# Loading q one head at a time: four transfers of 32 partitions instead of two of 64

## The chip, the cores and the metric

One core of one Trainium2 chip runs the kernel. The metric is the device time of one launch in microseconds (us), the median over several runs. All inputs and the output are float32 in the chip's HBM.

## The reference

With q, k, v of shape 8 x 8 x 576 x 64 (batch, head, position, head dimension):

```
kv  = einsum('bhsd,bhse->bhde', k, v)
out = einsum('bhsd,bhde->bhse', q, kv)
out = out / sqrt(mean(out * out, axis=-1) + 1e-6) * g_norm
x   = out with the heads side by side: 4608 x 512
h   = x @ w_in                       # 512 x 2048
g   = h * tanh(softplus(h))          # "mish"
result = g @ w_out                   # 2048 x 512
```

So there is a linear attention without a softmax, a norm over each head's 64 numbers, and a feed-forward part of two large products.

## The kernel before

The 4608 tokens are cut into nine tiles of 512 (`BLOCKS`, tile j). As a batch entry has 576 positions, a tile does not line up with the batches: `segments(j)` gives one segment (batch, first position, columns of the tile) for the tiles 0 and 8, and two for the tiles 1 to 7.

The work has two parts. In the first, tile after tile, TensorE multiplies x with w_in (L734 in tile 0, L780 later, products in a Strassen-like scheme of seven products a group; `gf` holds the x forms that are split into a high and a low part, `wfa` and `wfb` the same of w_in). ScalarE applies mish, and the results go by GpSimd's DMA queue to a buffer in HBM (`gd`, L818). In the second part, from about 531 us, they are read back and multiplied with w_out (L1148), and the result is stored.

While the products of tile j run, the attention of tile j + 1 is made in between. Its steps for each of two units u (four heads each):

- load (L452): q of the unit's four heads goes into `qs`, 128 partitions x 1024 numbers: a head takes 32 partitions, and a partition holds, for each segment, a run of consecutive numbers of its head. Unit 0 and unit 1 have a buffer each, which is free again when it has been transposed.
- transpose (L470): VectorE turns blocks of 32 x 32, `qs` into `fl` (unit 0) and `fm` (unit 1).
- project (L862): TensorE multiplies with the kv matrices of the batches (`kv`), made from k and v (loads `km`, `vm`, L344; products L371).
- square, sums, ln, exp: the norm, per token and head, into `fl`; keep (L567) and spread (L574) send it through HBM (`rd`) and back to all partitions of a head (`fh`, `fa`); normalize (L584) multiplies.
- the x forms (L200, L201) are made from that, and the next tile's products read them.

Between these steps the first tiles hold the conversion of w_in (load L242, scale L215, join L210 to L212, blocks and forms L200, L201) and the later ones that of w_out (load L224, stored again by GpSimd's queue, `wod`). Tile 0's q is loaded in another way (L432) and is not touched.

The order is written by hand: `WHEN`, `LATER`, `LATER0` and `LAST` give each step a slot among TensorE's products, and within each engine and each queue the instructions are issued in that order. All loads shown here, of q, k, v, the weights and the spread, are issued by SyncE (SP), one after the other; GpSimd's queue has the stores to `gd` and `wod`. An engine that waits for one instruction's input holds back all that stands behind it.

Of the kernel before, what the change touches and what calls it, by code (L numbers as in the profile page):

```python
# [36 lines left out]
def linear_attention_rms_mish_ffn(  # L37
# [34 lines left out]
    nc = tc.nc  # L72
    B, H, S, D = q.shape
# [4 lines left out]
    R = 32  # L78
# [20 lines left out]
    def start(j):  # L99
        return FIRST + NS * (j - 1) if j else 0  # L100
# [247 lines left out]
    def half(o, turned=False):  # L348

        o = 1 - o if turned else o  # L350
        return slice(o * D, (o + 1) * D)
# [33 lines left out]
    def quarter(p, m):  # L385
        return slice((2 * p + m) * R, (2 * p + m + 1) * R)
# [23 lines left out]
    def segments(j):  # L410

        segs, at_ = [], OFF[j]
        while at_ < OFF[j] + TS[j]:
            b, s0 = divmod(at_, S)
            n = min(S - s0, OFF[j] + TS[j] - at_)
            segs.append((b, s0, slice(at_ - OFF[j], at_ - OFF[j] + n)))
            at_ += n
        return segs
# [18 lines left out]
    def unit_steps(j, u):  # L437
# [4 lines left out]
        def load():  # L442


            t = qs[u] = att.tile([P, TM // R * D], F32, name=f"qs{u}")
            for b, s0, cols in segments(j):
                run = (cols.stop - cols.start) // R * D
                c0 = cols.start // R * D
                for o in range(2):
                    src = q[b, 4 * u + o, s0:s0 + 1, :]  # L450
                    src = bass.AP(src.tensor, src.offset, [[2 * S * D, 2], [run, R], [1, run]])
                    nc.sync.dma_start(t[half(o, u == 1), c0:c0 + run], src)  # L452

        def transpose(a=None):
            if j < T32:
# [130 lines left out]
        def projected():  # L586
            st["x2"] = x2_new()
            return st["x2"], st["q"]

        return {f.__name__: f for f in (projected, load, transpose, turned, project, square, scaled, sums, table, ln, exp, rstd, keep, spread, normalize)}  # L590


# [390 lines left out]
    for b in range(4, B):  # L983
        t = start(b - 2)
# [165 lines left out]
    def o_dst(st, block):  # L1150
        if "o" not in st:
            st["o"] = u_room("r", False, 2 * T).rearrange("p (r n) -> p r n", r=2)
        r, c = int(block[0]) - 1, int(block[1]) - 1
        return st["o"][:, r, c * G:(c + 1) * G]
# [77 lines left out]
    for i in range(NT):  # L1232
        for n in range(NQ):
            st = {"i": i, "n": n, "chunks": (2 * n, 2 * n + 1), "bank": bank_new, "take": nc.vector.tensor_copy if T32 <= i < NT - 1 and n in BY_DVE else nc.scalar.copy}
            t = start(i) + (7 if i else 8) * n
# [3 lines left out]
    t = start(NT)  # L1239
# [89 lines left out]
    o = o_dst(prev, "21")  # L1329
# [39 lines left out]
```

## Time and profile before

| | |
|---|---|
| median of 3 runs | 885.72 us (885.11 to 886.43) |
| the profiled execution | 887.06 us, its span 885.2 us |
| mean granted clock of TensorE | 0.958 |
| TensorE busy | 809.8 us, 91% of the span |
| VectorE busy | 595.6 us, 67% |
| ScalarE busy | 444.9 us, 50% |
| GpSimd busy | 109.1 us, 12% |
| DMA | 157.99 MB, mean 178 GB/s |

The profile is of one execution. Engines are named PE (TensorE's matmuls), PEld (its weight loads), DVE (VectorE), ACT (ScalarE), POOL (GpSimd) and SP (SyncE); a q behind the name means the engine's queue or sequencer. L452 is line 452 of the kernel, `qs<-in_q_dram` an instruction that writes qs and reads the input q, x60 the count. Times in rows of the timeline count from the start of the span. In a table of stretches, a row has the stretch, its length, the busy time of each engine with the number of instructions, the clock that TensorE was granted (1.00 is full speed), the mean busy share of the core's 16 DMA engines, and what these moved in GB/s.

### The profile page before, as it was taken

How to read it: one execution, taken by the hardware profiler on the slowest of the kernel's cores; microseconds unless marked ns; L12 is line 12 of the kernel's file. 1: busy time of each engine (PE TensorE's matmuls, PEld its weight loads, DVE VectorE, ACT ScalarE, POOL GpSimd, SP SyncE). 2: the span in 40 equal slices, each digit the busy share in tenths (PEclk: the TensorE clock that was granted, in tenths of full speed). 3: DMA queues.
4: the chain of work that ended last, by engine and by line, in shares of the span. 5: the costliest groups of instructions: out<-in, count | busy, mean ns of one | idle time of the engine just before them, and what ended most of it. 6: DMA issues, size and time to landing. Idle time of an engine off the chain costs nothing.

```text
span 885.2 us, 16602 instructions
## 1 busy us (share of the span) xinstructions
PE 809.8 (91%) x6764; PEld 730.4 (83%) x6764; DVE 595.6 (67%) x795; ACT 444.9 (50%) x688; POOL 109.1 (12%) x195
## 2 busy tenths in 40 slices
PE   7847879499897998889799999999999999999997
PEld 5635769489797997889689999888888888888887
DVE  3827754457554666474555489888888888788875
ACT  5626646164454655465364485454444544444452
POOL 2200101013131132233121110000000000000000
PEclk9977989799998999999899999999999999999999
DMA  9845815548476485656534996333334443343331
GB/s 305 284 140 187 249 62 162 180 147 296 171 272 216 157 271 176 199 179 240 179 108 157 360 315 265 117 121 127 133 121 138 169 145 119 120 143 120 126 113 49
DMA packets 63653, 157.99 MB, mean 178 GB/s; under 512 B 7384, under 2 KB 28120, under 8 KB 61272
## 3 DMA queue, kind: packets, MB, share of 16 engines
q1 hardware_dynamic: 49336, 109.92, 37.9%
q0 software_dynamic: 14144, 46.93, 14.2%
q8 instruction: 53, 0.87, 0.4%
q14 instruction: 24, 0.20, 0.1%
q10 hardware_dynamic: 96, 0.07, 0.0%
HBM read 100.40 MB, written 56.49 MB: 177 GB/s over the span
## 4 chain that ended last, share of the span: by engine, by line
PE 67%; DMA 24%; DVE 3%; SPq 3%; issue 1%; ACT 1%; DVEq 0%; POOL 0%; ACTq 0%
PE a L1148 21%; PE bc L1148 16%; PE a L780 14%; DMA qs<-in_q_dram 12%; PE bc L780 9%; DMA wfb<-in_moe_w_in_dram 7%; PE x L862 2%; PE q L1267 2%; DMA fh<-rd 2%; SPq L452 2%; DMA fa<-rd 1%; PE x L371 1%; DMA w<-in_moe_w_in_dram 1%; DMA gd<-u 1%; PE x L532 1%
## 5 line engine op out<-in xcount | busy, mean ns | idle before, releaser
L780 PE MATMUL a<-gf,wfb 128*128 128x256 f32 x1152 | 153.7, 288 | 2.3 <-DVE u L836 2.2
L200 ACT CAST gf<-g 128x1024 fp32r<-128x1024 f32 (+1 forms) x103 | 105.9, 1044 | 96.1 <-PE a L1148 50.5
L201 DVE TENSOR_TENSOR gf<-g,gf 128x1024 fp32r<-128x1024 f32 (+1 forms) x103 | 123.6, 1213 | 43.9 <-ACT gf L200 43.9
L780 PEld LDWEIGHTS a<-gf,wfb 128*128 128x128 f32 x1152 | 147.1, 197 | 5.6 <-DVE u L836 3.0
L1148 PE MATMUL a<-wfb,gf 128*128 128x512 f32 (+1 forms) x800 | 144.9, 337 | 0.0
L1148 PEld LDWEIGHTS a<-wfb,gf 128*128 128x128 f32 x800 | 125.4, 190 | 16.4
L1148 PE MATMUL bc<-wfb,gf 128*128 128x512 f32 (+1 forms) x544 | 98.0, 337 | 0.0
L1148 PEld LDWEIGHTS bc<-wfb,gf 128*128 128x128 f32 x544 | 82.6, 190 | 10.1
L818 POOL DMA_DIRECT2D gd<-u x96 | 57.0, 596 | 273.0 <-ACT u L197 228.5
L197 ACT ACTIVATE u<-u 128x1024 f32<-128x1024 f32 (+1 forms) x65 | 54.8, 843 | 69.9 <-DVE u L836 69.4
L836 DVE TENSOR_TENSOR u<-bc,u 128x512 f32<-128x512 f32 x64 | 43.1, 685 | 34.7 <-PE bc L780 30.2
L780 PE MATMUL a<-gf,wfa 128*128 128x256 f32 x384 | 54.7, 294 | 11.7 <-ACT u L694 11.7
L780 PEld LDWEIGHTS a<-gf,wfa 128*128 128x128 f32 x384 | 50.4, 200 | 17.4 <-ACT u L694 12.3
L780 PE MATMUL bc<-gf,wfa 128*128 128x256 f32 x384 | 53.9, 291 | 6.5 <-DVE u L836 4.2
L780 PEld LDWEIGHTS bc<-gf,wfa 128*128 128x128 f32 x384 | 50.2, 198 | 8.4 <-DVE u L836 4.7
L780 PE MATMUL bc<-a,wfb 128*128 128x256 f32 x384 | 52.5, 287 | 0.9 <-ACT u L686 0.9
L780 PE MATMUL bc<-gf,wfb 128*128 128x256 f32 x384 | 51.4, 283 | 0.0
L780 PEld LDWEIGHTS bc<-a,wfb 128*128 128x128 f32 x384 | 49.4, 196 | 2.3 <-issue 1.2
L1148 PE MATMUL bc<-wfa,gf 128*128 128x256 f32 (+1 forms) x272 | 50.3, 337 | 0.0
L1148 PE MATMUL a<-wfa,gf 128*128 128x256 f32 (+1 forms) x272 | 49.8, 336 | 0.0
L1148 PEld LDWEIGHTS a<-wfa,gf 128*128 128x128 f32 x272 | 44.1, 189 | 6.6
L780 PEld LDWEIGHTS bc<-gf,wfb 128*128 128x128 f32 x384 | 48.4, 192 | 0.1
(203 smaller groups left out, 1182.9 us busy)
## 6 DMA issues: line engine op xcount, KB each, us to landing
g<-gd SPq DMA_DIRECT2D x18, 2048.0 KB
gd<-u POOLq DMA_DIRECT2D x72, 256.0 KB, 5.6
gd<-u POOLq DMA_DIRECT2D x36, 512.0 KB, 6.7
w<-in_moe_w_out_dram SPq DMA_DIRECT2D x32, 256.0 KB
km<-in_k_dram SPq DMA_DIRECT2D x28, 288.0 KB
vm<-in_v_dram SPq DMA_DIRECT2D x28, 288.0 KB
wfb<-in_moe_w_in_dram SPq DMA_DIRECT2D x28, 256.0 KB
out_dram<-u SPq DMA_DIRECT2D x44, 128.0 KB
```

Source lines behind the costliest of these rows:

```text
L197: nc.scalar.activation(o, i, AF.Mish)
L200: nc.scalar.copy(hi, src)
L201: nc.vector.tensor_sub(lo, src, hi.bitcast(F32))
L371: nc.tensor.matmul(outs[a][half(o, a == 1)], kt[half(o), d], vt[half(o), d], start=(c == 0), stop=(c == 8))
L452: nc.sync.dma_start(t[half(o, u == 1), c0:c0 + run], src)
L532: nc.tensor.matmul(ss[j][hp * R:(hp + 1) * R, c], sel, sq[j, n][:, a, c], start=True, stop=True)
L780: nc.tensor.matmul(bank[:, jj], w[:, a, kc, :], xf[:, b, kc, :], start=first and jj == kc == s == 0, stop=(kc == 1 and s == 2), skip_group ...
L818: eng.dma_start(to, o)
L836: nc.vector.tensor_add(o, bank, o)
L862: nc.tensor.matmul(x2[half(o), a, cols], kvt[b % 2][r, m, u], of[r, c, m], start=m == 0, stop=m == 1)
L1148: nc.tensor.matmul(to, of, by, start=first and n == 0, stop=n == len(todo) - 1, skip_group_check=True)
L1267: nc.tensor.matmul(banks[b][:, h], gf[:, a, c, :], wo_form(2 * n + c, right)[:, :, d, :], start=n == c == s == h == 0, stop=last_one, skip ...
```

## The change

From the second tile on (tiles 1 to 8; tile 0 keeps its own load), a unit's four heads were loaded by two transfers for each segment, each of two heads into 64 partitions. Its source pattern has the two heads outermost, then 32 runs, then the numbers of a run. Now there are four transfers for each segment, one for each head, into 32 partitions each; the source pattern has the 32 runs outermost, which lie one behind the other in memory. The places in `qs` are the same: `half` gives 64 partitions, `quarter(p, m)` the m-th 32 of half p. The bytes are the same, too; the number of transfers of this line goes from 60 to 120, each of half the bytes.

```diff
             for b, s0, cols in segments(j):
                 run = (cols.stop - cols.start) // R * D
                 c0 = cols.start // R * D
-                for o in range(2):
-                    src = q[b, 4 * u + o, s0:s0 + 1, :]
-                    src = bass.AP(src.tensor, src.offset, [[2 * S * D, 2], [run, R], [1, run]])
-                    nc.sync.dma_start(t[half(o, u == 1), c0:c0 + run], src)
+                for h in range(4):
+                    src = q[b, 4 * u + h, s0:s0 + 1, :]
+                    src = bass.AP(src.tensor, src.offset, [[run, R], [1, run]])
+                    nc.sync.dma_start(t[quarter(h % 2 ^ u, h // 2), c0:c0 + run], src)
```

## The prediction

> **What bounds the kernel now.** I read the page first. Of its strips (40 slices of 22.1 us), the one of the granted clock and the one of DMA show that the second half is quiet: there TensorE runs at full clock, one matmul after the other. What can be won lies in the first 450 us, and there the chain of waits names one load again and again.
>
> ```profile
> span 885.2 us, 16602 instructions
> ...
> PE a L1148 21%; PE bc L1148 16%; PE a L780 14%; DMA qs<-in_q_dram 12%; PE bc L780 9%; DMA wfb<-in_moe_w_in_dram 7%; PE x L862 2%; PE q L1267 2%; DMA fh<-rd 2%; SPq L452 2%; DMA fa<-rd 1%; PE x L371 1%; DMA w<-in_moe_w_in_dram 1%; DMA gd<-u 1%; PE x L532 1%
> ```
>
> 12% of the chain is the load of q into qs, the very line of the change, and 2% its issue (SPq L452). The chain says what ended last, not what is lost; so next the waits (engine and line, what it waited for, us in all, times, longest):
>
> ```profile
> PE x L862 <- DVE fm L470: 21.9, 5, 5.4
> ...
> DVE fm L470 <- DMA qs<-in_q_dram: 12.5, 3, 6.4
> ...
> DVE fm L470 <- DMA w<-in_moe_w_out_dram: 11.2, 2, 6.2
> ```
>
> Five times TensorE stands still before the projection (L862), 21.9 us in all, because VectorE has not transposed the second q tile (fm). L470 reads nothing but qs, so whatever name stands behind it (a wait is put down to the last event), the load of q is what is late; VectorE takes its work in order and everything behind L470 waits too. The timeline shows three more stalls of that root (start, duration, engine, line, and in brackets the idle time before):
>
> ```profile
> 49.97 1.12 ACT L215 ACTIVATE wfa<-wfb 128x1024 f32<-128x1024 f32 x1 [10.94 <-DMA wfb<-in_moe_w_in_dram]
> 52.08 6.72 PE L734 MATMUL bc<-gf,wfb 128*128 128x512 f32 x18 [8.23 <-ACT wfb L200]
> 68.14 1.25 DVE L470 STREAM_TRANSPOSE fm<-qs 128x1024 f32<-128x1024 f32 x1 [10.62 <-DMA km<-in_k_dram]
> 72.07 4.63 PE L734 MATMUL a<-gf,wfb 128*128 128x512 f32 x10 [8.95 <-DVE wfb L201]
> 159.67 1.25 DVE L470 STREAM_TRANSPOSE fl<-qs 128x1024 f32<-128x1024 f32 x1 [8.60 <-DMA qs<-in_q_dram]
> 165.59 2.93 PE L780 MATMUL a<-gf,wfa 128*128 128x256 f32 x12 [6.62 <-ACT u L694]
> ```
>
> 6.62 us at 165.59 follow VectorE's block at 159.67; 8.95 us at 72.07 follow its block at 68.14, since the wfb split that TensorE wants stands behind that transpose. The 8.23 us at 52.08 wait for a w_in load issued right behind a q load.
>
> Why are loads of 512 KB late by 10 us? The DMA share in stretches in which a q load is all that is left (columns: PE, PEld, DVE, ACT, POOL busy, granted clock, DMA share, GB/s):
>
> ```profile
> 112.00:118.00 6.00, 1.51 (x12) 1.14 (x10) 0.38 (x1) 0.35 (x1) 0.00 (x0) 1.00 0.13 51
> 290.00:292.00 2.00, 2.00 (x19) 2.00 (x18) 1.97 (x2) 1.22 (x3) 0.00 (x0) 1.00 0.12 50
> ```
>
> 0.13 of 16 engines is 2.1 engines: a q load runs on two of the sixteen, at 50 GB/s. A unit's 512 KB takes 512 KB / 50 GB/s = 10.5 us alone, and on these two engines it stands behind, and ahead of, their sixteenth of everything else. Two is also the outermost count of the load's source pattern, its two heads; the change takes that count away.
>
> **The change part by part.** (1) Engines. Where the trace has no load of q on 32 partitions, the nearest row is the store of out, four transfers of 128 KB from 32 partitions each:
>
> ```profile
> 715.68 2.62 SPq L1187 DMA_DIRECT2D out_dram<-u  x4
> 717.00:718.00 1.00, 1.00 (x6) 0.82 (x5) 1.00 (x2) 0.00 (x0) 0.00 (x0) 1.00 0.89 207
> 718.00:719.00 1.00, 1.00 (x6) 0.80 (x5) 0.96 (x2) 0.39 (x1) 0.00 (x0) 1.00 0.84 199
> 719.00:720.00 1.00, 1.00 (x6) 0.84 (x5) 1.00 (x2) 1.00 (x2) 0.00 (x0) 1.00 0.52 119
> ```
>
> 0.89 of the engines, 207 GB/s, 512 KB in 3 us. Ends for a unit's load: 10.5 us (still two engines) and 3 us; I take 3 us, an estimate from the row with the same partitions and bytes. The Trainium skill, "DMA: Bandwidth & Descriptors", section "Why a DMA increments its semaphore by 16 and not by 1", gives the number of engines as the largest up to 16 that divides the size of the slowest dimension of both sides: 2 before, 16 after. The trace's 2.1 agrees for before; that loads of 32 partitions take 16, no row here shows. By it the lower end, and the sum as it stands, would be certain and rival D out; without it both stay open.
>
> (2) Issues. 15 segments in tiles 1 to 8, two units: 60 transfers become 120.
>
> ```profile
> L452 SPq DMA_DIRECT2D qs<-in_q_dram x60: 503/617/6659, 30.2 to 426.1; - x60
> 147.87 12.22 SPq L452 DMA_DIRECT2D qs<-in_q_dram  x4
> 256.27 8.75 SPq L452 DMA_DIRECT2D qs<-in_q_dram  x4
> 265.07 5.96 SPq L344 DMA_DIRECT2D km<-in_k_dram  x1
> 275.14 7.09 SPq L224 DMA_DIRECT2D w<-in_moe_w_out_dram  x4
> ```
>
> At the median 0.617 us that is 4 x 0.617 = 2.5 us more of SP's queue for a load of two segments, 37 us over the kernel. Behind it stand the k and v loads and the w_out loads. But SP now spends 12.22 us on four issues at 147.87 and 5.96 on one k load, since it waits for earlier transfers to land before it may issue more. With loads that land in 3 us most of this goes, so I price the issues at 0 in the middle tiles; bare, in the two early tiles, at 2 x 2.5 = 5 us.
>
> (3) Landing. In tile 5 the second unit is issued from 256.27 and transposed at 281.80. The engines' share falls in between:
>
> ```profile
> 266.00:268.00 2.00, 2.00 (x19) 2.00 (x18) 1.97 (x4) 1.40 (x2) 0.56 (x1) 1.00 0.59 214
> 268.00:270.00 2.00, 2.00 (x19) 2.00 (x18) 1.97 (x4) 1.24 (x3) 0.68 (x1) 1.00 0.27 107
> 281.80 1.25 DVE L470 STREAM_TRANSPOSE fm<-qs 128x1024 f32<-128x1024 f32 x1 [6.22 <-DMA w<-in_moe_w_out_dram]
> ```
>
> The other engines have run dry by about 270; with the work evenly spread all lands there, 5.6 us before VectorE comes to the transpose (281.80 - 6.22 = 275.58). The stall is covered. In tile 3 both units are late and the second has perhaps 1 to 2 us of cover; I leave 2 us there.
>
> (4) Stalls that go: 21.9 + 6.62 + 8.23 + 8.95 = 45.7 us.
>
> (5) The clock. After each of these stalls TensorE runs at half clock (columns: PE busy, granted clock, DMA share, GB/s):
>
> ```profile
> 52.08:56.60 4.52, 4.48 (x10) 0.50 0.68 179
> 72.07:77.10 5.03, 5.03 (x42) 0.50 0.87 267
> 118.92:124.90 5.98, 5.98 (x73) 0.50 0.02 6
> 165.59:169.30 3.71, 3.71 (x17) 0.51 0.97 270
> 175.97:179.50 3.53, 3.53 (x62) 0.50 0.77 243
> 230.35:234.10 3.75, 3.75 (x63) 0.55 0.36 111
> 283.10:288.70 5.60, 5.60 (x71) 0.50 0.48 172
> 335.59:339.90 4.31, 4.31 (x69) 0.61 0.35 114
> ```
>
> Busy time times (1 - clock): 2.2 + 2.5 + 3.0 + 1.8 + 1.8 + 1.7 + 2.8 + 1.7 = 17.5 us. No row shows the half clock without a stall ahead of it in these eight places, so I let it go with the stalls; if it stayed, the sum would be 17.5 us smaller.
>
> (6) What is late next. VectorE between the early stalls and in a later tile:
>
> ```profile
> 52.00:118.00 66.00, 49.02 (x530) 38.46 (x530) 39.73 (x56) 32.51 (x59) 5.32 (x9) 0.86 0.62 191
> 229.00:282.00 53.00, 48.23 (x552) 45.16 (x552) 31.02 (x51) 27.22 (x44) 12.54 (x21) 0.97 0.65 222
> 372.84 1.23 DVE L584 TENSOR_TENSOR gf<-gf,fh 128x1024 f32<-128x1024 f32 x1 [6.21 <-DMA fh<-rd]
> ```
>
> From 52 to 118 it is busy for 39.73 us; with the 8.95 us stall, the projection's longest (5.4, it ends at 118.92) and 4.7 us of half clock (2.2 + 2.5) gone, the stretch is 47 us and VectorE busy for 85% of it. In a later tile it is 31.02 of about 46 (53 less a stall of 4.4 and 2 to 3 of clock), 67%: no bound. For the early stretch I give back between 0 and 6 us (its idle time falls from 26 to 7 us, so most small waits of today must fit); I take 1.
>
> Sum: 45.7 + 17.5 - 5 (issues) - 2 (tile 3) - 1 (VectorE) = 55 us. The profiled execution took 887.06 us, its span 885.2; the median of the runs is 885.72, so 1.3 us below it. 887.06 - 55 is 832, and for the median 885.7 - 55 = 831 us.
>
> **The rivals.** (A) Other waits take over. At 372.84 VectorE idled 6.21 us for the norm's spread (fh<-rd), which SP issues behind w_out loads, and TensorE stalled though q was there. For it: the tiles get shorter, the spread's round trip does not. Against it: the spread and its reader lie after the projection, in a stretch that runs without a stall today, and no q wait lies inside it. If this eats the half of stalls and clock: 885.7 - 63.2 / 2 = 854 us; if only the five projection stalls go and the clock does not recover, 885.7 - 21.9 = 864.
>
> (B) More goes than I counted: w_out loads that wait behind q on SP come earlier too, and with them the spread at 372.84 and its like in the next tile, worth 6.2 us each and 2 us of clock. 885.7 - 63.2 - 8 = 814 us.
>
> (C) Slower: small transfers run one after another, and eight of them hold up SP. SP waits for landings before it issues more (12.22 us above). If a load of eight were served at the pace of eight issues under such waits, 8 x 12.22 / 4 = 24 us against 12 now, the w_out and k loads behind it come 12 us later; with 6 us of that covered, five tiles lose 6 us each: 886 + 30 = 916 us. It decides if one transfer of 32 partitions stays on two engines. The stores at 717 (four in 3 us) speak against it. The Trainium skill, "DMA: Bandwidth & Descriptors", section "Rules for kernel authors", speaks for it: it counsels one large transfer over many small ones, and says that two to disjoint partition halves serialize. No run here shows that.
>
> (D) The load stays on two engines and the added issues hide: 886 us, no change. The two heads of the source would then not be what confines it.
>
> **How the numbers follow.** What can be told from no change here is 0.2%, 1.8 us. My forecast, most of the stalls and clock gone: 0.58, 831 us, its own range 822 to 845. A: 0.22, around 854. B: 0.12, 814. C: 0.05. D: 0.03. Faster is the forecast with A and B, 0.92; same 0.03; slower 0.05. Leaving out C, D and the far end of B and A gives 814 to 862 us.
>
> **What would show it.** Right: no stretch at 0.13 and 50 GB/s while a q load is alone in flight; 120 issues at L452; L470 without idle time before it; the row "PE x L862 <- DVE fm L470" gone; full clock from 118 to 340; tiles of about 46 us where they took 53. Wrong: the row stays (the loads are still on two engines), or PE's idle time before the first product of a tile grows, put down to fh<-rd or to VectorE (A), or SP's issues at L452 take longer than 0.6 us each and the w_out loads start later after the projection than now (C).

## The result, and the profile after

| | before | after |
|---|---|---|
| median | 885.41 us (4 runs, 884.62 to 886.43) | 808.55 us (4 runs, 807.16 to 810.29) |
| ratio | | 0.9132, 95% interval 0.9109 to 0.9155 |
| profiled execution, its span | 887.06, 885.2 us | 809.48, 807.7 us |
| mean granted clock | 0.958 | 0.996 |

The kernel is 8.7% faster, 76.9 us. The forecast was 831 us with a range from 814 to 862: the direction and the main mechanism held, and the gain is 22 us larger than the sum, outside the range. First the page of the changed kernel (span, busy time, the chain of waits):

```profile
span 807.7 us, 16677 instructions
...
PE 785.2 (97%) x6764; PEld 716.5 (89%) x6764; DVE 595.2 (74%) x795; ACT 445.4 (55%) x688; POOL 108.5 (13%) x195
...
PE a L1148 23%; PE a L780 22%; PE bc L1148 18%; PE bc L780 16%; PE q L1267 2%; DMA w<-in_moe_w_in_dram 2%; PE x L862 2%; PE x L371 2%; DMA fh<-rd 1%; PE a L734 1%; PE x L532 1%; PE bc L734 1%; DMA wfb<-in_moe_w_in_dram 1%; DVE gf L584 0%; PE x L734 0%
```

The load of q has left the chain, where it had 12%, and its issue too. VectorE and ScalarE do the same work as before (595.6 and 444.9 us then). TensorE executes the same 6764 matmuls in 785.2 us instead of 809.8: 24.6 us less, which is the clock. It idles for 807.7 - 785.2 = 22.5 us, before for 885.2 - 809.8 = 75.4: 52.9 us less. The two make up the 77.5 us of the span.

What TensorE still waits for (engine and line, what it waited for, us in all, times, longest):

```profile
PE x L371 <- issue: 5.0, 3, 2.6
...
PE a L780 <- DVE u L836: 2.0, 2, 1.8
...
PE x L862 <- DVE kv L393: 1.5, 1, 1.5
```

The 21.9 us before L862 for VectorE's transpose are gone, and so are the waits of 8.95 and 8.23 us behind wfb. What is left is small and has other causes. Two of these rows are new or longer: before, the waits at L371 put down to issue came to 2.2 us, and L862 did not wait for kv. A wait that is not TensorE's own shrank as well, VectorE's for the norm's spread; the row of before, then the row of after:

```profile
DVE gf L584 <- DMA fh<-rd: 23.0, 6, 13.0
```

```profile
DVE gf L584 <- DMA fh<-rd: 7.2, 5, 2.4
```

The stretches after (columns as in the prediction):

```profile
52.00:104.00 52.00, 48.17 (x542) 39.48 (x546) 42.52 (x65) 38.93 (x65) 5.49 (x9) 1.00 0.70 221
...
150.00:196.00 46.00, 46.00 (x555) 44.26 (x555) 31.05 (x51) 26.37 (x44) 12.57 (x21) 1.00 0.76 253
```

A middle tile's 555 matmuls now take 46 us at full clock without a gap, where 552 took 53. Where the gain arises can be read from the starts of each tile's projection (first product at L862, us from the start of the span) and of the second part (first at L1148):

| tile | 1 | 2 | 3 | 4 | 5 | 6 | 7 | 8 | L1148 |
|---|---|---|---|---|---|---|---|---|---|
| before | 76.6 | 113.1 | 170.3 | 226.1 | 277.8 | 331.5 | 392.6 | 445.6 | 548.6 |
| after | 56.2 | 91.7 | 131.9 | 180.5 | 226.4 | 272.3 | 325.7 | 369.5 | 472.0 |
| ahead by | 20.4 | 21.4 | 38.4 | 45.6 | 51.4 | 59.2 | 66.9 | 76.1 | 76.6 |

The gain grows through all the tiles, and the second part adds next to nothing to it (0.9 us from there to the end of the span). The step to the eighth projection, 9.2 us, holds none of the eight stalls that the forecast named; so there is something that it had not counted.

### The profile page after: what moved, and what is told of

Read it like the earlier page. It is cut to its first block, busy times and chain, and to the rows that moved or that the text cites. A ratio compares the mean times of both kernels' runs of the same rounds, so it can differ in the third digit from the quotient of the medians.

```text
span 807.7 us, 16677 instructions
## 1 busy us (share of the span) xinstructions
PE 785.2 (97%) x6764; PEld 716.5 (89%) x6764; DVE 595.2 (74%) x795; ACT 445.4 (55%) x688; POOL 108.5 (13%) x195
## 3 DMA queue, kind: packets, MB, share of 16 engines
q0 software_dynamic: 14144, 46.93, 15.5%
## 4 chain that ended last, share of the span: by engine, by line
PE 89%; DMA 4%; DVE 3%; ACT 2%; issue 1%; SPq 1%; ACTq 0%; DVEq 0%
PE a L1148 23%; PE a L780 22%; PE bc L1148 18%; PE bc L780 16%; PE q L1267 2%; DMA w<-in_moe_w_in_dram 2%; PE x L862 2%; PE x L371 2%; DMA fh<-rd 1%; PE a L734 1%; PE x L532 1%; PE bc L734 1%; DMA wfb<-in_moe_w_in_dram 1%; DVE gf L584 0%; PE x L734 0%
## 5 line engine op out<-in xcount | busy, mean ns | idle before, releaser
L780 PE MATMUL a<-gf,wfb 128*128 128x256 f32 x1152 | 151.0, 285 | 2.0 <-DVE u L836 2.0
L780 PEld LDWEIGHTS a<-gf,wfb 128*128 128x128 f32 x1152 | 144.3, 194 | 4.2 <-DVE u L836 2.4
L1148 PE MATMUL a<-wfb,gf 128*128 128x512 f32 (+1 forms) x800 | 144.9, 337 | 0.0
L1148 PEld LDWEIGHTS a<-wfb,gf 128*128 128x128 f32 x800 | 125.4, 190 | 16.4
L1148 PE MATMUL bc<-wfb,gf 128*128 128x512 f32 (+1 forms) x544 | 98.0, 337 | 0.0
L1148 PEld LDWEIGHTS bc<-wfb,gf 128*128 128x128 f32 x544 | 82.6, 190 | 10.1
L780 PE MATMUL bc<-gf,wfa 128*128 128x256 f32 x384 | 51.8, 284 | 1.3 <-DVE gf L201 0.9
L780 PEld LDWEIGHTS a<-gf,wfa 128*128 128x128 f32 x384 | 48.3, 192 | 5.0 <-issue 4.2
L780 PE MATMUL a<-gf,wfa 128*128 128x256 f32 x384 | 51.9, 284 | 0.0
L780 PE MATMUL bc<-gf,wfb 128*128 128x256 f32 x384 | 51.4, 283 | 0.0
L780 PE MATMUL bc<-a,wfb 128*128 128x256 f32 x384 | 51.4, 283 | 0.0
L780 PEld LDWEIGHTS bc<-gf,wfa 128*128 128x128 f32 x384 | 48.4, 192 | 2.4 <-DVE gf L201 1.1
L1148 PE MATMUL bc<-wfa,gf 128*128 128x256 f32 (+1 forms) x272 | 50.3, 337 | 0.0
L1148 PEld LDWEIGHTS a<-wfa,gf 128*128 128x128 f32 x272 | 44.1, 189 | 6.6
L1148 PE MATMUL a<-wfa,gf 128*128 128x256 f32 (+1 forms) x272 | 49.8, 336 | 0.0
L200 ACT CAST gf<-a 128x1024 fp32r<-128x1024 f32 x17 | 17.9, 1055 | 57.0 <-DVE a L1092 57.0
L780 PEld LDWEIGHTS bc<-a,wfb 128*128 128x128 f32 x384 | 48.4, 192 | 0.6 <-issue 0.6
```

The lines of the kernel that those rows point to most:

```text
L200: nc.scalar.copy(hi, src)
L780: nc.tensor.matmul(bank[:, jj], w[:, a, kc, :], xf[:, b, kc, :], start=first and jj == kc == s == 0, stop=(kc == 1 and s == 2), skip_group ...
L1148: nc.tensor.matmul(to, of, by, start=first and n == 0, stop=n == len(todo) - 1, skip_group_check=True)
```

## The experiments

All are edits of the changed kernel, run in rounds with the kernel before. Differences below are those of the medians, from 808.55 us; taken from the ratios to the kernel before, which was run beside each, they come out up to 2.3 us smaller or 1.0 us larger. The first three bring rows of q into other partitions than the attention needs, so they can only be read for their time. Where both forms of the load stand in one kernel, the lines behind it move: L567, L574, L584, L780 and L862 become L573, L580, L590, L786 and L868 there. Two questions were open: is it the outermost count of the source pattern that matters, or the size and number of the transfers; and which loads hold the 22 us that the sum lacks.

### 120 transfers of 32 partitions, but two heads in each

```diff
-                    src = q[b, 4 * u + h, s0:s0 + 1, :]
-                    src = bass.AP(src.tensor, src.offset, [[run, R], [1, run]])
+                    src = q[b, 4 * u + h % 2, s0:s0 + 1, :]
+                    src = bass.AP(src.tensor, src.offset, [[2 * S * D, 2], [run, R // 2], [1, run]])
```

> 120 transfers into 32 partitions each, of the same bytes and run lengths as after the change, but each names two heads with 16 runs of each (source pattern 2 x 16 x run): which rows of q land in a partition is changed, the amount is not. Theory (the outermost count of the source pattern sets the number of DMA engines, two before): the loads are on two engines again, share 0.13 and 50 GB/s where a q load is alone, the stalls at the projection (21.9 us in five before) are back, and the time is that of before or above, 885 to 905 us, since there are 60 issues more. Rival (smaller transfers, 32 partitions, more of them in flight made it): 806 to 815 us, as after the change (808.6).

Measured: 880.14 us, ratio 0.9947 (0.9926 to 0.9968), 5 us below the range that I expected. The issues, TensorE's waits, and a stretch in which q (0.14 MB of the 0.21) and the rest of a GpSimd store are all that moves:

```profile
L452 SPq DMA_DIRECT2D qs<-in_q_dram x120: 604/605/3127, 29.3 to 421.5; - x120
```

```profile
PE x L862 <- DVE fm L470: 21.2, 5, 5.6
```

```profile
284.00:288.00 4.00, 4.00 (x36) 4.00 (x35) 3.14 (x5) 2.67 (x6) 0.56 (x1) 1.00 0.13 52
```

Number, size and destination of the transfers are those of the change, and yet nearly all of the gain is gone: the five stalls are back, and all that moves uses 0.13 of the engines, 52 GB/s, as before. The 60 added issues of 0.6 us each do not make the kernel slower; it is 0.5% faster than before.

### 60 transfers of 64 partitions, one stretch of 64 runs in each

```diff
-                for h in range(4):
-                    src = q[b, 4 * u + h, s0:s0 + 1, :]
-                    src = bass.AP(src.tensor, src.offset, [[run, R], [1, run]])
-                    nc.sync.dma_start(t[quarter(h % 2 ^ u, h // 2), c0:c0 + run], src)
+                for o in range(2):
+                    src = q[b, 4 * u + o, s0:s0 + 1, :]
+                    src = bass.AP(src.tensor, src.offset, [[run, 2 * R], [1, run]])
+                    nc.sync.dma_start(t[half(o, u == 1), c0:c0 + run], src)
```

> 60 transfers into 64 partitions, as many and as large as before the change, but each names one stretch of 64 runs of memory (source pattern 64 x run), so that the second 32 partitions get the next positions of the first head and not the other head. Theory (outermost count): 16 engines, 805 to 811 us, as after the change or up to 3 us less, since 60 issues go. Rival (size and number of transfers): 885 us, as before.

Measured: 809.9 us, 0.9159 (0.9141 to 0.9178). The number and size of the transfers of before give the time of after, once the outermost count is 64. With the first experiment this answers the question: neither the number nor the size of the transfers makes the gain, the source's outermost count does. What is left is that one stretch of memory was read instead of two; the next experiment speaks against that, since with four separate heads the share follows the count.

### 30 transfers of 128 partitions, four heads outermost

```diff
-                for h in range(4):
-                    src = q[b, 4 * u + h, s0:s0 + 1, :]
-                    src = bass.AP(src.tensor, src.offset, [[run, R], [1, run]])
-                    nc.sync.dma_start(t[quarter(h % 2 ^ u, h // 2), c0:c0 + run], src)
+                src = q[b, 4 * u, s0:s0 + 1, :]
+                src = bass.AP(src.tensor, src.offset, [[S * D, 4], [run, R], [1, run]])
+                nc.sync.dma_start(t[:, c0:c0 + run], src)
```

> 30 transfers into all 128 partitions, each names four heads (source pattern 4 x 32 x run), in the order of the heads and not in that of the change, so rows stand in other partitions. Theory (outermost count): four engines, share 0.25 and 100 GB/s where a q load is alone, 512 KB in 5.2 us; the slack of about 5 us that I had reckoned covers most of it: 809 to 825 us. Rival 1 (all counts under 16 are as bad as two): 860 to 890 us. Rival 2 (few large transfers are best, the outermost count does not matter): 803 to 808 us and a share above 0.5.

Measured: 821.31 us, 0.9283 (0.9262 to 0.9304), as expected. A stretch with q alone (but for one packet of k or v), and TensorE's longest wait (this kernel's lines are one lower):

```profile
70.00:72.00 2.00, 2.00 (x10) 1.67 (x9) 0.54 (x2) 2.00 (x4) 0.00 (x0) 1.00 0.27 100
```

```profile
PE a L733 <- DVE wfb L201: 6.6, 2, 6.2
```

Four heads outermost give twice the share and twice the rate of two: 0.13 and 50 GB/s, 0.27 and 100 GB/s, so 25 GB/s for an engine. That already saves 64 of the 77 us; about half of the rest is the early stall behind wfb. The Trainium skill, "DMA: Bandwidth & Descriptors", section "Why a DMA increments its semaphore by 16 and not by 1", gives the largest number up to 16 that divides the slowest dimension of both sides; both shares agree with it.

### 240 transfers, each run halved

```diff
                 for h in range(4):
-                    src = q[b, 4 * u + h, s0:s0 + 1, :]
-                    src = bass.AP(src.tensor, src.offset, [[run, R], [1, run]])
-                    nc.sync.dma_start(t[quarter(h % 2 ^ u, h // 2), c0:c0 + run], src)
+                    for w in range(2):
+                        src = q[b, 4 * u + h, s0:s0 + 1, :]
+                        src = bass.AP(src.tensor, src.offset + w * run // 2, [[run, R], [1, run // 2]])
+                        cw = c0 + w * run // 2
+                        nc.sync.dma_start(t[quarter(h % 2 ^ u, h // 2), cw:cw + run // 2], src)
```

> As after the change, but each transfer is cut in two along its runs: 240 transfers of half the bytes, runs of 256 B to 2 KB. It doubles the cost that I had priced as issues (rival C of the prediction). Theory (engines decide, issues hide): 808 to 815 us. Rival (the number of transfers costs): each load of two segments takes 16 issues of 0.35 to 0.45 us, 3 us more of SP's queue; if a third of 15 loads show it, +15 us, 824 us or above.

Measured: 820.29 us, 0.9274 (0.9253 to 0.9296): above what I expected, and below the 824 us of the rival. SP's issues in the first tile of this kernel, and TensorE's longest wait:

```profile
29.66 9.21 SPq L454 DMA_DIRECT2D qs<-in_q_dram  x16
...
42.98 11.10 SPq L454 DMA_DIRECT2D qs<-in_q_dram  x16
54.22 2.71 SPq L242 DMA_DIRECT2D wfb<-in_moe_w_in_dram  x4
```

```profile
PE bc L736 <- ACT wfb L200: 3.1, 1, 3.1
```

So issues are not free without limit: two loads of 16 hold SP for 20 us (5.6 of them are waits for earlier transfers to land), and the w_in blocks behind them start at 54.22 us where they start at 45.44 us after the change. Halving the runs makes them shorter as well as more; the two are not told apart. A second kernel halves the runs from tile 3 on only (the inner loop runs over `range(2 if j > 2 else 1)`).

> Transfers of half runs (16 instead of 8 a load of two segments) from tile 3 on, the form of the change in tiles 1 and 2. With half runs everywhere the time was 820.3 us, and its trace has 5.8 us of stalls around 44 to 60 that the change has not. Theory (the extra issues cost only where a load that TensorE waits for stands right behind q on SP, the w_in loads of tile 1): 808 to 813 us. Rival (each extra transfer costs the same wherever it is): 13 of 15 segments are in tiles 3 to 8 or so, 817 to 820 us.

Measured: 811.48 us, 0.9171 (0.9134 to 0.9209). Of the 11.7 us that halving cost, about 3 are left, and the interval meets that of the change. The price of halving is paid in the two early tiles, where SP's queue also feeds w_in; later it is nearly all hidden.

### The old form in some of the loads

These keep the change and put the two heads back in a part of the loads, by a condition:

```diff
+                if not old:            # the condition differs, see below
                     for h in range(4):
                         ...
+                else:
+                    for o in range(2):
+                        src = q[b, 4 * u + o, s0:s0 + 1, :]
+                        src = bass.AP(src.tensor, src.offset, [[2 * S * D, 2], [run, R], [1, run]])
+                        nc.sync.dma_start(t[half(o, u == 1), c0:c0 + run], src)
```

Old in tiles 1 and 2 (`j <= 2`):

> The new loads from tile 3 on, the old ones in tiles 1 and 2. Theory (each stall belongs to its own load, and the half clock to the stall before it): the three early stalls of 8.23, 8.95 and 5.4 us come back with 2.2 + 2.5 + 3.0 us of half clock, and the 1.4 us of stall and 1.7 us of half clock around 107: 808.6 + 33 = 842, within 836 to 848 us. Rival (the early tiles are bound by VectorE or by DMA as a whole, and the gain there came from elsewhere): under 825 us.

Measured: 836.69 us, 0.9435 (0.94 to 0.9471), as expected. TensorE's waits:

```profile
PE bc L740 <- ACT wfb L200: 7.1, 1, 7.1
PE a L740 <- DVE wfb L201: 6.7, 2, 6.3
PE x L868 <- DVE fm L476: 5.7, 1, 5.7
```

Of the eight stalls the three early ones are back, and they alone; 28 of the 77 us belong to these two tiles.

Old in unit 0 of all tiles (`u == 0`), and old in unit 1 of all tiles (`u == 1`):

> The new loads for unit 1, the old ones for unit 0. Theory: what comes back is what hung on unit 0, the 8.23 us of the w_in load behind the first unit 0 load and the 6.62 us behind the unit 0 transpose of tile 3, with 2.2 + 1.8 us of half clock: 808.6 + 19 = 827, within 815 to 835 us. Rival (two engines full with half of the q bytes still hold up everything): above 845 us.

> The new loads for unit 0, the old ones for unit 1. Theory: the five stalls at the projection (21.9 us) and the 8.95 us behind the unit 1 transpose of tile 1 stay with 13.5 us of half clock: 808.6 + 44 = 853, within 843 to 865 us; its gain and that of the run with unit 1 new add up to the 77 us of both within 10 us. Rival (half of the bytes on two engines is little enough for the loads to land in time): under 830 us.

Measured: 842.46 us (0.9497, 0.9453 to 0.9542) with unit 0 old, 7 us above my range, and 863.45 us (0.9736, 0.9692 to 0.978) with unit 1 old, within it. TensorE's waits, unit 0 old, then unit 1 old:

```profile
PE bc L740 <- ACT wfb L200: 7.7, 1, 7.7
PE a L786 <- ACT u L700: 6.9, 2, 6.0
PE bc L786 <- DVE u L842: 5.4, 2, 3.8
```

```profile
PE x L868 <- DVE fm L476: 25.9, 6, 6.4
PE a L740 <- DVE wfb L201: 10.8, 2, 10.4
```

The stalls before L862 are the second unit's, as its name fm says. But unit 0, for which no product waits directly, costs 34 us: the early wfb (7.7 us) and the wait of tile 3 (6.0 us), as expected, and beyond these 6.2 us around 330 to 341 and 3.4 us around 386 to 390 us at L786, where VectorE's and ScalarE's own work is late. The next four runs take these late groups apart.

Old in tiles 7 and 8 (`j >= 7`):

> The new loads in tiles 1 to 6, the old ones (two heads a transfer) in tiles 7 and 8. In the kernel before, TensorE stalled for 6.4 us between 369 and 388 and for 6.0 us between 422 and 435, with 4.2 us of half clock, though q was there; after the change most of that is gone, and my prediction had not counted it. Theory (inherited: these stalls came from the q loads of tiles 5 and 6, which held up SP and the w_out loads and so the spread behind them): 808 to 814 us. Rival (they came from the loads of tiles 7 and 8 themselves, which share two engines with the spread): 820 to 826 us, with the same stalls.

Measured: 823.54 us, 0.9289 (0.9258 to 0.932). I had held that the waits at the starts of the products of tiles 6 and 7 were inherited from earlier tiles, and that these late loads were hidden. That fell, and the rival came true: 15 us of the gain (14 by the ratios) come from the loads of these two tiles. TensorE's timeline (start, duration, and in brackets the idle time before):

```profile
312.75 1.70 PE L786 MATMUL bc<-gf,wfa 128*128 128x256 f32 x12 [2.06 <-DVE u L842]
...
362.08 2.01 PE L786 MATMUL a<-gf,wfa 128*128 128x256 f32 x12 [3.71 <-ACT u L700]
```

These are two groups, and they stand in the trace of before as well:

```profile
377.62 2.93 PE L780 MATMUL bc<-gf,wfa 128*128 128x256 f32 x12 [3.92 <-DVE u L836]
```

```profile
426.04 2.93 PE L780 MATMUL a<-gf,wfa 128*128 128x256 f32 x12 [4.03 <-ACT u L694]
```

Old in tile 7 alone (`j == 7`):

> The old loads in tile 7 alone, the new ones elsewhere. With the old loads in tiles 7 and 8, TensorE stalled for 6.0 us around 310 to 323 and for 6.6 us around 358 to 371. Theory (each group belongs to the load that is in flight then, tile 7's to the first, tile 8's to the second): 813 to 819 us, the second group is gone. Rival (the delay is handed on from tile to tile along the chain of w_out stores and loads): 820 to 825 us, both groups stay.

Measured: 814.16 us, 0.9202 (0.9172 to 0.9232), as expected. Only the first group is left, with one wait of 4.5 us; the second belongs to tile 8's load.

Old in one load of all, unit 0 of tile 8 (`j == 8 and u == 0`), two transfers of 256 KB:

> Of the changed kernel only one load goes back to two heads: unit 0 of tile 8, two transfers of 256 KB in all the kernel (L452, issued at about 336 us). Its own data are wanted only some 50 us later. Theory: what hurts is not this load's own landing but the keep step of tile 7 (L580, rd<-fl, 4 KB with an outermost count of two), which is issued some 4 us behind it and stands on the same two engines; then rd<-fl takes 12 to 18 us from issue to landing instead of about 4, the spread fh<-rd starts at about 356 us instead of 341, the products of tile 7 stall again at 358 to 371 us by some 5 to 6.5 us with half clock behind them, and the time is 814 to 819 us. Rival: the second group of stalls in the kernel with old tiles 7 and 8 came from unit 1's load, or from SP's queue; then the 4 KB land as in the changed kernel, no stall comes back, and the time is 807 to 811 us.

Measured: 818.94 us, 0.9224 (0.9168 to 0.928), at the upper end of what I expected. Two transfers out of all cost 10 us (8 by the ratios), by the far and near ends of both kernels' intervals between 1 and 15; the stall that the theory asks for is there. SP's issues, first the changed kernel, then this one:

```profile
336.85 1.12 SPq L567 DMA_DIRECT2D rd<-fl  x4
339.59 1.20 SPq L224 DMA_DIRECT2D w<-in_moe_w_out_dram  x2
340.95 1.26 SPq L574 DMA_DIRECT2D fh<-rd  x2
```

```profile
332.54 1.70 SPq L458 DMA_DIRECT2D qs<-in_q_dram  x2
336.69 1.22 SPq L573 DMA_DIRECT2D rd<-fl  x4
343.24 1.23 SPq L224 DMA_DIRECT2D w<-in_moe_w_out_dram  x2
353.21 1.28 SPq L580 DMA_DIRECT2D fh<-rd  x2
```

What SP waited for from 330 to 360 us, and what VectorE and TensorE did then:

```profile
SPq L580 <- DMA rd<-fl: 8.6, 2, 8.3
```

```profile
358.73 1.23 DVE L590 TENSOR_TENSOR gf<-gf,fh 128x1024 f32<-128x1024 f32 x1 [11.66 <-DMA fh<-rd]
```

```profile
357.11 1.69 PE L786 MATMUL a<-gf,wfa 128*128 128x256 f32 x12 [2.13 <-ACT u L700]
363.51 2.93 PE L786 MATMUL bc<-gf,wfa 128*128 128x256 f32 x12 [3.28 <-DVE u L842]
```

Keep (L573 here; the expectation wrongly calls it L580, which is the spread) is issued at the same time in both, 336.7 and 336.9 us. Its transfers are `nc.sync.dma_start(rd[j][2 * n:2 * n + 2], st["r"][n * R:n * R + 2])`, 4 KB each from two partitions, so their outermost count is two as well. Behind the two-head load SP may issue the spread 16.5 us after keep, without it 4.1 us after: 8.3 us of the difference are its wait for the 4 KB to land, and 3.7 us the w_out load ahead of the spread, which comes later too (343.24 against 339.59). VectorE then idles 11.66 us at the normalize step, and TensorE 2.13 + 3.28 us with its products. The load's own reader, the transpose at 363.98 us (31 us after the issue, not 50), waits for nothing. In the kernel before, the same four rows:

```profile
399.55 1.70 SPq L452 DMA_DIRECT2D qs<-in_q_dram  x2
403.72 1.39 SPq L567 DMA_DIRECT2D rd<-fl  x4
411.06 1.26 SPq L224 DMA_DIRECT2D w<-in_moe_w_out_dram  x2
421.51 1.27 SPq L574 DMA_DIRECT2D fh<-rd  x2
```

17.8 us from keep to spread, with an 8.7 us wait for the 4 KB.

The traces also record each packet's start, queue and size, and these can be told apart by size. After the change the load's 128 packets of 4 KB start between 333.1 and 336.0 us, and keep's eight of 2 KB from 337.9 to 339.2. With the two heads back the load's packets start between 336.1 and 351.6 us, and keep's only from 350.9 to 352.5, 14 us after its first issue. The w_out load is issued behind keep and spread over all engines: of its 512 packets 448 start between 344.6 and 347.6, ahead of keep's, and 64 only from 351.8 on. 64 of 512 are two sixteenths. So most of the engines were free for work issued after keep, and keep's packets moved when those of the w_out load on two engines did: both stood behind the q load. In the kernel before it is the same: q from 403.4 to 420.1, keep from 419.7, and 448 and 64 packets of w_out, the 64 from 420.0 on.

The Trainium skill, in the section named above, says that a transfer which SP issues onto fewer engines takes the lowest-numbered ones; by that keep and the q load stand on the same two. The packets agree; no run here shows the numbers of the engines, and a keep on other engines was not tried.

### Old in tiles 7 and 8, issued by ScalarE

```diff
-                        nc.sync.dma_start(t[half(o, u == 1), c0:c0 + run], src)
+                        nc.scalar.dma_start(t[half(o, u == 1), c0:c0 + run], src)
```

> As with the old loads in tiles 7 and 8 alone (823.5 us, ratio 0.9289), but these old loads are issued on ScalarE's queue, so that SP issues nothing of them and waits for none of them. Theory (two full engines: every store and load that is spread over all 16 ends with these two, so w_out's stores, its next loads and the spread come late): 816 to 826 us, the stalls behind VectorE at the start of tiles 7 and 8 stay. Rival (SP held up: the w_out loads and the spread wait in SP's queue behind the issues of q): 806 to 812 us.

Measured: 859.46 us, 0.9706 (0.9675 to 0.9738), 33 us above the range that I expected. This one does not answer its question. The transpose of tile 7's second unit:

```profile
348.35 1.25 DVE L476 STREAM_TRANSPOSE fm<-qs 128x1024 f32<-128x1024 f32 x1 [16.88 <-DMA qs<-in_q_dram]
```

ScalarE issues in step with its own work, so the load was late from the start (issued from 330.31 us, where SP issues it at 301.97 us after the change), and the stall it makes is another. It shows one thing directly: from the first issue to the transpose a two-head load of a unit takes 18.0 us here, where 10.5 us had been worked out for it alone; the four issues take 3.65 us of that, and other transfers are in flight.

## Why the prediction came out too high

**Engines (1): right.** Two heads outermost, two engines; runs outermost, many more. The first three experiments show it from both sides. The 3 us that the sum took for a unit's 512 KB were right as well: 2.9 us from the first to the last packet of tile 8's first unit, 15.5 us with its two heads back. That all sixteen are used was not seen by itself. One reading behind it was loose. The stretches of the prediction do not hold q alone: from 112 to 118 us 29 of some 100 packets on SP's queue are of k or v, and from 290 to 292 a GpSimd store has 0.06 of the 0.10 MB. The 0.13 is what q and the last shares of spread transfers use together on the two engines that are still busy. From 80.2 to 85 us of the kernel before q does stand alone (the DMA queues, all that moved: packets, MB, share of 16 engines), and the share is the same:

```profile
q1 hardware_dynamic: 141, 0.23, 13.3%
```

Rival D (the load stays on two engines) is out, and with it C: eight transfers do not run one after another.

**Stalls that go (4): right.** All eight are gone, 45.7 us, and the row of L862 with them. What remains for L470 is no wait at all.

**Issues (2): right in size at SP, in part by luck, and wrong at the end.** The queue in the first tile, before and after:

```profile
30.21 2.76 SPq L452 DMA_DIRECT2D qs<-in_q_dram  x4
...
38.15 6.32 SPq L344 DMA_DIRECT2D vm<-in_v_dram  x1
44.51 6.17 SPq L452 DMA_DIRECT2D qs<-in_q_dram  x4
50.79 10.33 SPq L242 DMA_DIRECT2D wfb<-in_moe_w_in_dram  x4
```

```profile
30.27 5.43 SPq L452 DMA_DIRECT2D qs<-in_q_dram  x8
...
39.05 6.14 SPq L452 DMA_DIRECT2D qs<-in_q_dram  x8
45.44 2.51 SPq L242 DMA_DIRECT2D wfb<-in_moe_w_in_dram  x4
```

The first load takes SP 2.7 us more, as priced (2.5). But the price was four more issues of 617 ns; an issue now takes 345 ns at the median, and of the 11.6 us of both loads 5.3 are waits for earlier transfers to land. But SP is no longer held up at a v load (6.32 us) and at the w_in blocks (10.33 us, now 2.51), so these blocks are issued 5.4 us earlier, not later. I had used that argument for the middle tiles and not for the early ones, although the trace had it there too. The 5 us given back do not show at this place.

**Landing in tile 3 and VectorE (3, 6): too careful.** Neither the 2 us nor the 1 us shows where it was expected. From 52 to 104 us VectorE is busy for 42.52 of 52 us, 82%, and the longest of TensorE's waits there are 1.45 us for kv and 1.35 us before a product at L371. The three small terms together, 8 us, are a third of the miss. Small waits did grow elsewhere: outside the eight stalls and the two groups below, TensorE idles 3.1 us longer than before.

**The clock (5): right, and short by 7.1 us.** 17.5 us were taken from eight stretches; TensorE's busy time fell by 24.6. Of the rest 2.5 us belong to the two groups below, where 4.2 us were lost before and 1.7 are still lost (313.9 to 319 us, clock 0.67); the other 4.6 lie in smaller pieces, 2 us of them ahead of 52 us. A stretch of before that was not in the list:

```profile
426.00:431.00 5.00, 4.96 (x23) 4.96 (x24) 3.77 (x7) 0.48 (x1) 0.56 (x1) 0.50 0.86 227
```

**What is late next (6): the step that failed.** The forecast put at nothing what would go of the two groups of stalls at the starts of the products of tiles 6 and 7 (369 to 388 and 422 to 436 us), because q was there. They came to 12.4 us of idle time and 4.2 us of half clock. After the change 2.1 us of idle time and the 1.7 us of clock are left, all in the first group: 12.8 us less. The experiment that puts the loads of tiles 7 and 8 back gives 15 us. I had the row in hand (372.84, 6.21 us idle for fh<-rd) and left it in the forecast as something that stays; rival B, which let it go, had 814 us. B's event is right, and its cause in part. In the second group the w_out load ahead of the spread does come earlier, by 3.7 us of 12.3, but the larger part is keep's 4 KB behind the q load, which B did not name. At 372.84 itself, in the first group, keep is not what was waited for: from keep to spread it took 11.4 us before and 8.6 after, most of it SP's wait for a w_out store to land ahead of the w_out load, and from the spread's issue to the normalize step 8.4 and 6.4 us. B's size was short too, 8 us against 12.8 to 15.

From the two profiles the whole is 45.7 (stalls) + 17.5 (their clock) + 12.8 (the two groups) + 4.6 (clock elsewhere) - 3.1 (small waits that grew) = 77.5 us; the forecast had the first two and took 8 off. That 831 less 8 and less the 15 of the experiment comes out at 808, so near the measured 808.55, is in part luck, since the last two terms nearly cancel.

**Rival A**, other waits that take over, was wrong in its direction: the waits for the spread did not grow with shorter tiles, they fell from 23.0 to 7.2 us; in the one place that was taken apart they hung on the q load themselves. Transfers that are spread over all engines came faster as well, which fits the two sixteenths of each that stand on the two busy ones (DMA issues: transfers, KB each, median us from issue to landing; before, then after):

```profile
wod<-w POOLq DMA_DIRECT2D x16, 256.0 KB, 5.5
```

```profile
wod<-w POOLq DMA_DIRECT2D x16, 256.0 KB, 3.2
```

The sizes of the parts do not add up exactly: 28 us for tiles 1 and 2 and 15 for 7 and 8 leave 34 for the tiles 3 to 6, which no run measured by themselves; the new loads in unit 0 alone gain 23 us and in unit 1 alone 44, 67 together, where both at once gain 77 (within the 10 us that I had allowed). How the load of tile 7 makes the first group late is shown only by the group's return: there keep was not held up for long, but the spread landed later (VectorE idle for 6.85 us at 309.66 us in that kernel, 2.15 us after the change).

## What to carry to other kernels

Look at the share of DMA engines in a stretch where one transfer is alone in flight, and check by the queues' packets that it is: here a share of 0.13 or 0.27 went with an outermost count of two or four, and one transfer for each head, with the runs outermost, mended it. (At the same number of transfers the time was as good, but the rows then stand in other partitions; a reordering of the pattern that keeps the places was not tried.) Price such a load not only by who reads it, but by everything that has a part on the same engines, the smallest transfers first; a stall elsewhere that "was there anyway" may hang on it. And when a queue is held up by landings, count what added issues cost only after taking away the hold-up that goes.

## What the runs showed of the hardware that I had not expected

Transfers of 4 KB moved only 14 us after their issue, and the step behind them could be issued 16.5 and 17.8 us after it, since they stood behind 512 KB on two engines; of a load spread over all engines the same two held back 64 of 512 packets. An issue of one plain stretch of runs holds SP for a shorter time than one with the heads outermost, 345 ns at the median against 605 ns with the same partitions, bytes and number (the first experiment):

```profile
L452 SPq DMA_DIRECT2D qs<-in_q_dram x120: 310/345/1127, 30.3 to 356.2; - x120
```

From one issue to the next it is more like 0.5 to 0.7 us (5.43 us for eight in the first tile), so the gain at the queue is smaller than the two medians suggest. The single stretch of 64 runs into 64 partitions took 596 ns at the median, so what sets this price is not settled.
